# A Sinkhorn-sorted attention followed by a token mixer: Sinkhorn on 128 partitions, another first V, no gates, and a new written-out order

## The chip, the cores and the metric

The kernel runs on one core of a Trainium2 chip. The time is the device time of one execution in microseconds (us); for the kernel before, three runs were taken, and their median is 125.45 us (125.16 to 125.81). The engines are PE (matrix multiply; PEld is its weight load), DVE (vector), ACT (scalar), POOL (GpSimd) and SP (which only issues DMAs here). PE writes to PSUM, eight banks of 128 partitions by 2 KB, and what it has written there is evicted to SBUF by ACT or DVE.

## The reference

There are B=4 batches, H=8 heads, S=768 tokens, D=64 per head, and 8 blocks of 96 tokens.

```python
P = sort_net                                   # (B, H, 8, 8)
for _ in range(5):
    P = exp(P - max(P, axis=-1))
    P = P / (sum(P, axis=-1) + 1e-09)          # rows
    P = P / (sum(P, axis=-2) + 1e-09)          # columns
k_sorted = einsum('bhij,bhjcd->bhicd', P, k_blocks)
v_sorted = einsum('bhij,bhjcd->bhicd', P, v_blocks)
scores = q_block @ k_sorted_block.T / sqrt(D)  # inside each block of 96
attn = exp(scores - max) / (sum + 1e-09)
x = attn @ v_sorted_block                      # -> (B, S, 512), heads side by side
# token mixer
W = (x @ w_q) @ (x @ w_k).T / sqrt(64)
out = relu(W @ x) @ w_out
```

Inputs and output are fp32; the matmuls of the kernel are bf16. The mixer is computed as q (k^T x), so no 768 by 768 matrix is made.

## The kernel before

**Layout.** A token index s is held as s = 6p + r, with p the partition (128 of them) and r from 0 to 5, so a block of 96 tokens covers 16 partitions times 6. The 8x8 matrix P of a head becomes a 128x128 matrix M (tile M, function `u_n`): the block mixing of all 16 partitions of each block at once. One M per head serves all r.

**Units.** The work is cut into some 440 small units. Each is a function `u_X`, and the string ORDER lists every unit in the order in which it is given to its engine; each engine runs its own units strictly in that order. An item such as `K216` is: function K, batch 2, index 1, PSUM bank 6. A small letter is the eviction of the unit of the same name, and its last letter is the engine: `k21A` evicts on ACT, `k21D` on DVE; `P` is POOL, `S` is SP. For a batch:

- `l`: a load. POOL issues a DMA that casts fp32 to bf16 on the way: all of q, k or v of a batch (768 KB written each), into three rotating buffers Qn, Kn, Vn (line 100).
- `Q`/`q`: transposes of q into QT, three units of 16 matmuls, 1024 columns each eviction.
- `K`/`k`: sorted and transposed k into KT, a pair of heads a unit (12 matmuls, 768 columns evicted).
- `V`/`v`: sorted v into Vs, token-major, three units of 8 matmuls and 1024 columns. `R` (line 271): six SP DMAs for each batch that regroup Vs into VT, where the 96 tokens of a block lie on 96 partitions.
- `S`/`e`: scores of five (block, head pair)s, and the exponential on ACT into E (line 301; seven units for a batch, the last with 384 columns, the others with 960).
- `P`, `r`, `x`: E by VT, with a column of ones that gives the sum; reciprocal and product on DVE into X (lines 328 and 333; five units, the last smaller).
- `T`/`t`, `J`/`j`, `W`/`w`, `G`/`g`, `H`/`h`, `O`/`o`, `y`: transposes of X, both projections, the transposed k part, k^T x (tile Ab), the mixed and rectified tile mixT, the output projection (6 units of four 128x512 matmuls; tile ot) and the store by SP (two rows r a store). `d` moves half of qkT to the other partitions (qD), mostly by an SP DMA.

**Sinkhorn** (`u_c`, lines 150 to 163) lies on 32 partitions, one for each (batch, head), with the 8x8 matrix along the free dimension. A round is one exponential on ACT and six DVE instructions: sum, reciprocal and product by rows, then by columns. Behind the fifth round `U`, `b`, `B` and `n` turn P and spread it into M: for batch 0 on DVE, for the others on POOL (`n`), from a copy of the spread P in SBUF (PTR).

**Fillers and gates.** `Z` units multiply zeros (tile fil, 64 matmuls of 128x512 in all) where PE would idle. `N` units are gates: POOL copies one element of a tile, so that it waits there, and the loads behind it in its queue start no earlier.

Of the kernel before, what the change touches and what calls it, by code (L numbers as in the profile page):

```python
# [14 lines left out]

ORDER = """
l00P l01P l02P i00P i03P i02P l11P c00D Z087 c01D i01D c02D Z027 c03D Z127 c04D Q026 Q007 q02D c05D
Q015 Z224 q01A q00D U006 Z423 b00D Z322 B003 n00D u00A Z522 n11P n01D Z622 K010 K032 n10P k01A K024  # L20
k03D Z727 k02A N02k l03P Z1026 V000 V022 v00A K004 v02D V016 k00A N00k l12P l10P Z821 R01S n21P v01D
R00S K112 S000 R04S S044 n20P e00A k11D S066 e06A R02S K100 e04A S012 R05S S036 R03S k10A Z1125 Z924
e03A K120 K134 e01A k12D S026 e02A k13D P002 S050 r00D Z1227 e05A x00D N00x l21P P014 V106 r01D P030
x01D v10A P042 r04D P024 r03D x04D T007 x03D V112 t00A R10S v11A r02D Q106 x02D R11S Q127 T031 q12A
Q110 q10D T015 t03D q11A N11q l20P l31P l04P l32P l30P T024 V122 t01A S100 n31P v12D S156 t02A J005
e10A n30P S122 R12S j00D J014 R15S e15A K200 R14S j01D W005 R13S e12A w00D W014 S116 w01D G005 e11A
K232 G015 k23A K216 g01D k20A k21D S144 P112 e14A P100 r11D K226 x11D P134 k22A r10D Q213 r13D x10D
S166 Q202 q21A x13D T101 q20A Q220 t10D S134 e16A q22D e13A K322 P146 k32D S250 S214 e25A r14D P122
x14D e21A K330 r12D S246 d00S x12D k33A K304 e24A k30D S220 T123 T112 e22A t12D K314 S236 t11D T133
k31A S260 J102 t13D e23A S204 d01S j10D J113 e26A N26e l22P e20A V306 V310 v30D j11A W102 H024 v31A  # L30
W113 w11D V326 w10D h02D G103 v32A H000 d10S R30S Q312 h00D Q325 q31A G113 q32D Q304 g11A H010 O057
q30D h01A S312 o05D S324 e31A S330 O036 R34S e32A R35S V222 o03D R33S O007 e33A v22D R32S d11S V214
R31S V200 o00D v21A R25S S342 O016 R24S v20D e34A R23S H114 R22S O027 o01D R20S R21S H100 P322 o02A
h11D y00S O046 h10A r32D S304 x32D y01S o04A O107 e30A P240 y02S P232 o10A r24D P214 x24D P226 r23D
r21D O131 x23D O120 r22D o13A x21D T233 o12A P201 x22D t23A S364 y11S O110 e36A r20D T223 x20D o11A
T217 P304 t22A y10S T202 r30D t21A H120 x30D J213 t20A P316 j21D h12A S354 J202 r31D d21S x31D e35A
W213 O141 j20D T300 w21D o14A d20S P334 t30D W207 P342 r33D O156 w20D x33D G207 o15A r34D T311 x34D
T320 y12S t31A G217 t32D T336 g21A J301 t33D H222 H214 j30D J310 h22A d30S W301 H206 j31A w30D O243
h20A d31S W312 G301 o24D h21A O250 w31D O227 o25A G311 y22S o22A O230 g31A H302 H324 o23A O211 h32A
y21S H316 O200 o21D O351 h30D h31A O345 o20A o35D O314 y20S o34D O307 o31A y32S O325 o30A O334 y30S  # L40
o32A o33A y31S
# [4 lines left out]
def kernel(  # L46
# [20 lines left out]
    D1 = D + 1  # L67
    DM = moe_w_out.shape[0]
    DH = moe_w_q.shape[1]
    PT = DM // P  # L70
    NU = NB * H
    TH = 5
    NT = -(-NB * NP // TH)
    EW = 2 * TH * BLK + P - BLK
    AG = 14
# [15 lines left out]
    Pm = sb.tile([BH, NB + 1, NB], FP32, name="Pm")  # L91
    nc.sync.dma_start(out=Pm[:, 0:NB, :], in_=sort_net.rearrange("b h i j -> (b h) i j"))
# [6 lines left out]
    def load(t, src, b):  # L99
        nc.gpsimd.dma_start(out=t[b % NIN].rearrange("p h r d -> p h (r d)"),  # L100
                            in_=src[b].rearrange("h (p r) d -> p h (r d)", p=P))

    QT = tiles("QT", 2, [P, NP, R6, P])
    KT = tiles("KT", 2, [P, NP, S + P - BLK])
    Vs = tiles("Vs", 2, [P, R6, H, D1])
    VT = tiles("VT", 2, [BLK, NB, H * D1])
    E = tiles("E", 2, [BLK, NT, EW])
    X = tiles("X", 2, [BLK, NB, DM])
# [6 lines left out]
    NOT = 4  # L115
    ot = tiles("ot", NOT, [P, 2, DM], FP32)
    M = tiles("M", 2, [P, H, SP, NB])
    R = tiles("R", 4, [BLK, 2, 7], FP32)
    PTR = sb.tile([P, NB, BH], BF16, name="PTR")
    Pb = sb.tile([BH, NB, NB], BF16, name="Pb")  # L120
    PbT = sb.tile([NB * NB, BH], BF16, name="PbT")
    Lx = sb.tile([NB * NB, NB, NB, SP], BF16, name="Lx")
    tmp = sb.tile([BH, NB], FP32, name="tmp")
# [4 lines left out]

    Pv = Pm[:, 0:NB, :]

    def rows(t):
        return t.unsqueeze(2).to_broadcast([BH, NB, NB])

    def cols(t):
        return t.unsqueeze(1).to_broadcast([BH, NB, NB])
# [12 lines left out]


    def u_c(b, n, e):  # L150
        if n == 0:
            nc.vector.memset(Pm[:, NB:NB + 1, :], 1e-9)
            nc.vector.memset(fil, 0.0)  # L153
            nc.vector.reduce_max(tmp, Pv, axis=AX.X)
            nc.vector.tensor_sub(Pv, Pv, rows(tmp))
            return
        nc.scalar.activation(Pv, Pv, ACT.Exp)
        nc.vector.reduce_sum(tmp, Pv, axis=AX.X)
        nc.vector.reciprocal(tmp, tmp)
        nc.vector.tensor_mul(Pv, Pv, rows(tmp))  # L160
        nc.vector.reduce_sum(tmp, Pm.rearrange("p i j -> p j i"), axis=AX.X)
        nc.vector.reciprocal(tmp, tmp)
        nc.vector.tensor_mul(Pb if n == 5 else Pv, Pv, cols(tmp))


    def u_i(b, n, e):
        if n == 0:
            nc.gpsimd.memset(idb, 0.0)
            nc.gpsimd.affine_select(out=idb, in_=idb, compare_op=ALU.not_equal, fill=1.0, base=0,
                                    pattern=[[-1, P]], channel_multiplier=1)  # L170
        elif n == 1:
            nc.vector.reduce_max(m_p, idb.rearrange("p (j s) -> p s j", s=SP), axis=AX.X)
        elif n == 3:
            nc.gpsimd.memset(Lx, 0.0)
            nc.gpsimd.affine_select(out=Lx.rearrange("p i j s -> p (i j) s"),
                                    in_=Lx.rearrange("p i j s -> p (i j) s"),
                                    compare_op=ALU.not_equal, fill=1.0, base=0,
                                    pattern=[[-1, NB * NB], [0, SP]], channel_multiplier=1)
        elif n == 2:
            for t in Vs:  # L180
                nc.gpsimd.memset(t[:, :, :, D:D1], 1.0)
            for t in KT:
                nc.gpsimd.memset(t[:, :, S:S + P - BLK], 0.0)
            for t in E:
                nc.gpsimd.memset(t[:, :, 2 * TH * BLK:EW], 0.0)
                nc.gpsimd.memset(t[:, NT - 1, 2 * (NB * NP - TH * (NT - 1)) * BLK:EW], 0.0)


    def u_l(b, n, e):
# [5 lines left out]
        else:  # L195
            load((Qn, Kn, Vn)[n], (q, k, v)[n], b)


    def u_U(b, n, bank):
        mm(bf(bank)[0:NB * NB, 0:BH], Pb.rearrange("p i j -> p (i j)"), idb[0:BH, 0:BH], t=True)  # L200

    def u_b(b, n, e):
        nc.vector.tensor_copy(PbT, bf(U["t"])[0:NB * NB, 0:BH])

    def u_B(b, n, bank):
        for i in range(NB):
            mm(PS[:, bank, i * BH:(i + 1) * BH], Lx[:, i].rearrange("p j s -> p (j s)"), PbT)

    U = {}

    def u_n(b, n, e):
        h0, h1 = n * 4, n * 4 + 4
        if b == 0:
            src = PS[:, U["bank"], 0:NB * BH].rearrange("p (i h) -> p h i", h=BH)
        else:
            src = PTR.rearrange("p i h -> p h i")
        src = src[:, b * H + h0:b * H + h1, :]
        ENG[e].tensor_tensor(  # L218
            out=M[b % 2][:, h0:h1], in0=src.unsqueeze(2).to_broadcast([P, 4, SP, NB]),
            in1=m_p.unsqueeze(1).unsqueeze(3).to_broadcast([P, 4, SP, NB]), op=ALU.mult)  # L220

    def u_u(b, n, e):
        copy(e, PTR.rearrange("p i h -> p (i h)"), PS[:, U["bank"], 0:NB * BH])


    def u_Z(b, n, bank):
        for _ in range(n):
            mm(PS[:, bank, :], fil[:, 0:P], fil)


    def u_Q(b, n, bank):
        ps = bf(bank).rearrange("p (k r s) -> p k r s", k=NP, r=2)
        for r in range(2):
            for kp in range(NP):
                for hh in range(2):
                    mm(ps[hh * D:(hh + 1) * D, kp, r, :], Qn[b % NIN][:, 2 * kp + hh, 2 * n + r, :],
                       idb, t=True)

    def u_q(b, n, e, bank):
        copy(e, QT[b % 2][:, :, 2 * n:2 * n + 2, :].rearrange("p k r s -> p k (r s)"),  # L240
             bf(bank).rearrange("p (k s) -> p k s", k=NP))


    def flat(bank, nb=2):
        return PS[:, bank:bank + nb, :].rearrange("p a n -> p (a n)")

    def u_K(b, n, bank):
        ps = flat(bank)
        for r in range(R6):
            for hh in range(2):  # L250
                h = 2 * n + hh
                mm(ps[hh * D:(hh + 1) * D, r * P:(r + 1) * P], Kn[b % NIN][:, h, r, :],
                   M[b % 2][:, h].rearrange("p s i -> p (s i)"))

    def u_k(b, n, e, bank):
        copy(e, KT[b % 2][:, n, 0:S].rearrange("p (i s r) -> p i s r", i=NB, s=SP),
             flat(bank)[:, 0:S].rearrange("p (r s i) -> p i s r", r=R6, s=SP))


    def u_V(b, n, bank):  # L260
# [209 lines left out]
```

## Time and profile before

| | |
|---|---|
| median of the runs | 125.45 us |
| span of the profiled execution (first to last instruction) | 123.3 us |
| PE busy, its mean granted clock | 101.9 us (83%), 0.934 |
| DVE busy | 69.5 us (56%), 132 instructions |
| ACT busy | 69.2 us (56%), 93 instructions |
| POOL busy | 27.1 us (22%) |
| casting loads (q0) | 10.09 MB written, 56.9% of the DMA engines' time |
| plain DMAs (q1) | 9.89 MB, 24.2% |
| fillers that the profile shows | 60, 17.6 us of PE |

A busy share is a mean over stages with different limits, and PE's busy time counts the depth of the pipeline with each matmul, and fillers too. So the page tells who is busiest and not what sets the time; for that the stretches of the span are read one by one. Granted clock 1.00 is full speed of PE. The page's GB/s count what is written; a casting load reads twice that from memory.

### The profile page before, as it was taken

What the parts mean: (1) busy time and instruction counts of PE and PEld (TensorE: products, weight loads), DVE (VectorE), ACT (ScalarE), POOL (GpSimd) and SP (SyncE); (2) the same over time, 40 slices, a digit from 0 to 9 for tenths busy, and PEclk for the clock granted to TensorE, in tenths of its full rate; (3) what the DMA queues carried; (4) which work ended last, traced back from release to release, by engine and by line L of the source; (5) the groups of instructions that cost most, each with busy time, mean ns of one, the idle gap of its engine ahead of it and who ended that gap; (6) DMA issues with size and microseconds to landing.
All of it is one profiled execution on the core that took longest, in us unless ns stands there. A gap on an engine that the chain in (4) does not pass through costs nothing. (4 is left out here: it accounts for less than half of the span.)

```text
span 123.3 us, 3389 instructions
## 1 busy us (share of the span) xinstructions
PE 101.9 (83%) x1439; PEld 65.7 (53%) x1449; DVE 69.5 (56%) x132; ACT 69.2 (56%) x93; POOL 27.1 (22%) x42
## 2 busy tenths in 40 slices
PE   5818877692799999608998999999999999999940
PEld 2216464541447886508887677554767665443410
DVE  2879547305402976404769669497697885304500
ACT  4113155863301699900579977885669736855550
POOL 6993096910020029900000030000000000000000
PEclk9976999999679999995589999999999999999995
DMA  0999999899949426999999339947947104144493
GB/s 4 141 203 203 205 203 153 142 215 227 147 34 203 106 57 57 196 243 206 206 203 206 54 33 175 260 104 202 396 156 308 53 16 175 32 169 171 167 363 153
DMA packets 19950, 20.19 MB, mean 164 GB/s; under 512 B 2016, under 2 KB 18400, under 8 KB 19936
## 3 DMA queue, kind: packets, MB, share of 16 engines
q0 software_dynamic: 14064, 10.09, 56.9%
q1 hardware_dynamic: 5872, 9.89, 24.2%
q8 instruction: 11, 0.18, 0.6%
q14 instruction: 3, 0.02, 0.1%
HBM read 20.19 MB, written 6.29 MB: 215 GB/s over the span
## 5 line engine op out<-in xcount | busy, mean ns | idle before, releaser
L301 ACT ACTIVATE E<-ps 96x960 bf16<-96x960 f32 (+1 forms) x28 | 24.2, 906 | 7.7 <-PE ps L138 7.6
L138 PE MATMUL ps<-wo,mixT 128*128 128x512 bf16 x90 | 22.6, 380 | 0.6 <-issue 0.2
L333 DVE TENSOR_TENSOR X<-ps,R 96x896 bf16<-96x896 f32 (+1 forms) x20 | 19.7, 998 | 0.5
L138 PE MATMUL ps<-fil 128*128 128x512 bf16 x60 | 17.6, 438 | 2.0 <-DVE fil L153 1.2
L138 PE MATMUL ps<-VT,E 96*128 96x65 bf16 x256 | 11.7, 202 | 7.7 <-DMA VT<-Vs 7.2
L138 PEld LDWEIGHTS <-E 96*128 96x128 bf16 x256 | 10.3, 103 | 9.4 <-issue 8.5
L142 ACT COPY ot<-ps 128x512 f32<-128x512 f32 x16 | 9.4, 585 | 10.1 <-PE ps L138 9.2
L138 PEld LDWEIGHTS <-mixT 128*128 128x128 bf16 x96 | 8.2, 98 | 9.4 <-issue 1.3
L328 DVE RECIPROCAL R<-ps 96x14 f32<-96x14 f32 (+1 forms) x20 | 4.3, 222 | 15.4 <-PE ps L138 15.4
L138 PEld LDWEIGHTS <-fil 128*128 128x128 bf16 x64 | 6.5, 110 | 10.0 <-issue 4.4
L138 PE MATMUL ps<-idb,Qn 128*64 128x128 bf16 x192 | 9.2, 263 | 3.1 <-DMA Qn<-in_q_dram 3.1
L142 ACT CAST KT<-ps 128x768 bf16<-128x768 f32 x9 | 7.1, 800 | 6.8 <-PE ps L138 6.8
L142 ACT CAST Vs<-ps 128x1024 bf16<-128x1024 f32 x6 | 6.2, 1029 | 8.1 <-PE ps L138 7.8
L144 DVE CAST KT<-ps 128x768 bf16<-128x768 f32 x7 | 6.6, 956 | 6.7 <-PE ps L138 6.5
L138 PE MATMUL ps<-M,Kn 128*64 128x128 bf16 x192 | 8.3, 227 | 2.2 <-DMA Kn<-in_k_dram 0.9
L138 PEld LDWEIGHTS <-Qn 128*64 128x64 bf16 x192 | 7.7, 138 | 4.3 <-DMA Qn<-in_q_dram 3.6
L138 PE MATMUL ps<-QT,KT 64*128 64x96 bf16 x256 | 9.8, 207 | 0.2 <-ACT KT L142 0.2
L144 DVE COPY ot<-ps 128x512 f32<-128x512 f32 x8 | 5.5, 689 | 7.6 <-ACT ot L142 4.8
L406 ACT ACTIVATE mixT<-ps 128x1024 bf16<-128x1024 f32 x8 | 8.1, 1029 | 2.7 <-PE ps L138 2.6
L144 DVE CAST Vs<-ps 128x1024 bf16<-128x1024 f32 x6 | 7.2, 1222 | 3.0 <-PE ps L138 3.0
L138 PEld LDWEIGHTS <-Kn 128*64 128x64 bf16 x192 | 6.4, 113 | 4.5 <-issue 2.5
L218 POOL TENSOR_TENSOR M<-PTR,m_p 128x512 bf16<-128x512 bf16 x6 | 7.7, 1321 | 5.0 <-ACT PTR L142 4.9
(67 smaller groups left out, 132.9 us busy)
## 6 DMA issues: line engine op xcount, KB each, us to landing
out_dram<-ot SPq DMA_DIRECT2D x12, 512.0 KB, 2.8
VT<-Vs SPq DMA_DIRECT2D x24, 130.0 KB, 4.6
Qn<-in_q_dram POOLq DMA_DIRECT2D x4, 768.0 KB, 11.0
Kn<-in_k_dram POOLq DMA_DIRECT2D x4, 768.0 KB, 10.9
Vn<-in_v_dram POOLq DMA_DIRECT2D x4, 768.0 KB, 11.5
wo<-in_moe_w_out_dram POOLq DMA_DIRECT2D x1, 512.0 KB, 14.7
qD<-qkT SPq DMA_DIRECT2D x8, 48.0 KB, 2.3
wqk<-in_moe_w_q_dram POOLq DMA_DIRECT2D x1, 64.0 KB, 3.5
```

The costliest lines, as they stand in the source:

```text
L138: nc.tensor.matmul(o, w, x, is_transpose=t, start=start, stop=stop, skip_group_check=True)
L142: nc.scalar.copy(o, i)
L144: nc.vector.tensor_copy(o, i)
L218: ENG[e].tensor_tensor(out=M[b % 2][:, h0:h1], in0=src.unsqueeze(2).to_broadcast([P, 4, SP, NB]), in1=m_p.unsqueeze(1).unsqueeze(3).to_bro ...
L301: nc.scalar.activation(E[b % 2][:, n, 0:2 * w * BLK].rearrange("p (t a c) -> p a t c", a=2, c=BLK), PS[0:BLK, bank:bank + 2, 0:w * BLK].re ...
L328: nc.vector.reciprocal(rr[b, n][:, :, 0:w], avps(bank, w)[:, :, :, D])
L333: nc.vector.tensor_mul(xo.rearrange("p (a t d) -> p a t d", a=2, d=D), avps(bank, w)[:, :, :, 0:D], rr[b, n][:, :, 0:w].unsqueeze(3).to_br ...
L406: nc.scalar.activation(o, i, ACT.Relu)
```

## The change

The diff replaces ORDER whole and changes the units as follows.

- **Sinkhorn** (`c`, `f`, `r`, `C`) lies on 128 partitions, one for each (batch, head, row i) of two batches; two groups (batches 0 and 1; 2 and 3) take turns. Of a round, `f` is the exponential with the row sum as a by-product, `r` reciprocal and product by rows on DVE, `C` two small fp32 matmuls on PE that sum the columns (a block-diagonal matrix of ones, blk, and a rank-one term for the 1e-9), `c` reciprocal from PSUM and product. POOL makes blk with a memset and two selects (`i04P`).
- **M** (`U`, `u`, `m`) comes from one transpose of the spread P for each group; all 16 products for M are on DVE, a pair of heads (256 columns) each.
- **First loads.** The first four heads of q and k of batch 0 are loaded as fp32 by SP into ot, which is free then, and cast head by head (`z`): six on POOL, one on DVE, one on ACT. The other halves, and v in two halves, are casting loads.
- **First V.** For batch 0 (TURNED) v is sorted and transposed like k, into VS (in the same memory as Vs), then turned back by eight PE transposes for a pair of heads (`A`) and evicted into VT (`a`, 1024 columns). Batch 0 has no `R` any more.
- **Pairs.** Q, S, P, X, T and J go by head pairs: Q and T are four units of 768 columns, J gathers as T units come, W turns all 128 columns where it turned 64.
- **Output.** ot is one tile with eight slots; the last batch's last two rows are stored singly.
- **Gates and fillers.** No gate is left in ORDER, and of the fillers 17 (13 of 128x512, 4 of 128x128), all ahead of `U001`.

```diff
-l00P l01P l02P i00P i03P i02P l11P c00D Z087 c01D i01D c02D Z027 c03D Z127 c04D Q026 Q007 q02D c05D
...
+i03D c00D l06S l05S i15P f01A r01D l08P i00P i01D i04P l07P f11A Z050 C010 c01D r11D f02A r02D
+Z031 Z111 C020 c02D f03A C111 c11D r03D z05P f12A r12D Z032 C031 l010P c03D f04A r04D C120 c12D
+f13A Z022 Z132 C041 c04D f05A r05D Q020 C051 q02A z00D Q032 l09P c05D z04P U001 r13D C130 z03A
+m01D V013 z01P c13D z02P m00D u00D q03A m03D v01A Q012 z06P z07P V005 q01D K010 V033 f14A r14D
+C142 v00D k01A m02D S020 v03A c14D A017 e02A A003 a00D f15A V024 a01D K000 K022 m10D r15D v02A
+Q006 q00D K034 A037 l10P i02P m12D k00A S010 k02A A022 k03A a03D S064 e01A a02D S046 Q113 q11D
...
+x00D v10A R11S V112 v11A P010 x01D P034 V126 v12A R14S R12S R15S x03D S032 e03A T000 U101 l11P
+K126 u10A K104 k12A K112 R13S k11A R10S t00D l03P k10D P040 x04D K136 k13A P024 S122 e12A S156
+T030 e15A m20D i25P S142 x02D T024 t03D t02D T015 t01D S136 e14A S110 e13A e11A m22D J002 J012
...
+J106 J116 J126 J136 R22S S204 j11D j10A H012 m33D h01A e20A l32P R20S R25S P240 x24D m31D W106
...
-    Pm = sb.tile([BH, NB + 1, NB], FP32, name="Pm")
+    Pm = sb.tile([P, 2, NB], FP32, name="Pm")
+    nc.sync.dma_start(out=Pm, in_=sort_net.rearrange("(g b) h i j -> (b h i) g j", g=2))
...
+    def u_c(g, n, e, bank=None):
...
+        c, p1, o = cs[:, g, :], Pm[:, g, :], Ue[:, g, 0:NB]
+        nc.vector.reciprocal(c, PS[:, bank, 0:NB])
+        if n == 5:
+            c, p1 = (t.unsqueeze(2).to_broadcast([P, NB, SP]) for t in (c, p1))
+            o = Pf[g]
+        nc.vector.tensor_mul(o, p1, c)
+
+    def u_f(g, n, e):
+        nc.scalar.activation(Uf[:, g, :], Ue[:, g, :], ACT.Exp, accum_out=rs[:, g:g + 1])
+
+    def u_r(g, n, e):
+        nc.vector.reciprocal(rs[:, g:g + 1], rs[:, g:g + 1])
+        nc.vector.tensor_scalar_mul(Pm[:, g, :], Uf[:, g, 0:NB], rs[:, g:g + 1])
+
+    def u_C(g, n, bank):
+        mm(PS[:, bank, 0:NB], eps[:, 0:P], eps[:, P:P + NB], stop=False)
+        mm(PS[:, bank, 0:NB], blk, Pm[:, g, :], start=False)
...
+    def u_m(b, n, e, bank):
...
+        ENG[e].tensor_tensor(
+            out=M[b % 2][:, 2 * n:2 * n + 2],
...
+    def u_z(b, n, e):
+        t = (Qn, Kn)[n // 4][0][:, n % 4].rearrange("p r d -> p (r d)")
+        src = ot.rearrange("p a n -> p (a n)")[:, n * R6 * D:(n + 1) * R6 * D]
...
     def u_V(b, n, bank):
+        if b in TURNED:
+            sort_turn(b, n, bank, Vn)
+            return
...
+    def u_A(b, n, bank):
+        ps = bf(bank).rearrange("p (i d) -> p i d", d=P)
+        for i in range(NB):
+            mm(ps[0:BLK, i, :], VS[b % 2][:, n, i * BLK:(i + 1) * BLK], idb, t=True)
+
+    def u_a(b, n, e, bank):
+        copy(e, VT[b % 2][:, :, 2 * n:2 * n + 2, 0:D],
+             bf(bank)[0:BLK].rearrange("p (i h d) -> p i h d", i=NB, h=2))
```

## The prediction

> **What bounds the kernel now.** I read the stretches of the span first (time, busy time per engine with the number of instructions in brackets, granted clock, DMA share, rate), cut where the behaviour changes.
>
> ```profile
> 24.00:31.20 7.20, 4.27 (x49) 2.26 (x49) 1.82 (x2) 3.55 (x5) 1.01 (x1) 1.00 1.25 221
> 31.20:38.50 7.30, 7.06 (x46) 3.39 (x48) 1.33 (x2) 0.97 (x1) 1.11 (x2) 0.77 0.79 108
> 51.30:55.80 4.50, 0.02 (x1) 0.00 (x0) 0.54 (x1) 1.10 (x2) 1.22 (x1) 1.00 1.24 238
> 55.80:62.20 6.40, 6.35 (x100) 5.40 (x102) 3.66 (x6) 2.49 (x3) 0.00 (x0) 0.50 1.28 205
> 62.20:72.30 10.10, 9.73 (x209) 7.67 (x208) 7.54 (x13) 9.28 (x13) 1.08 (x2) 0.98 0.84 132
> 72.30:118.60 46.30, 45.41 (x549) 26.42 (x552) 30.44 (x49) 31.18 (x43) 0.04 (x1) 1.00 0.58 173
> ```
>
> The columns are PE, weight loads, DVE, ACT, POOL. From 72.3 on PE is dense and sets the pace. Before that there are holes, and DVE and ACT starve with PE. The waits and PE in order of time say what the holes are:
>
> ```profile
> PE ps L138 <- DMA VT<-Vs: 7.2, 2, 4.5
> ...
> 24.21 3.18 PE L138 MATMUL ps<-fil 128*128 128x512 bf16 x13 [0.18 <-ACT E L301]
> ...
> 31.23 0.61 PE L138 MATMUL ps<-VT,E 96*128 96x65 bf16 x14 [2.72 <-DMA VT<-Vs]
> ...
> 33.04 5.60 PE L138 MATMUL ps<-fil 128*128 128x512 bf16 x20 [0.22 <-issue]
> ...
> 55.85 1.70 PE L138 MATMUL ps<-VT,E 96*128 96x65 bf16 x28 [4.53 <-DMA VT<-Vs]
> ...
> 112.38 6.22 PE L138 MATMUL ps<-wo,mixT 128*128 128x512 bf16 x27
> ```
>
> Both holes are the sorted V of a batch, regrouped by six DMAs from Vs to VT. For batch 0 PE idles or runs fillers from 24.2 to 38.5; for batch 1 it idles 4.5 us and then runs at half clock until 62.2. So the span is four pieces: 15.0 to the first sorted matmul (Sinkhorn and M), 57.3 with holes, 46.3 dense, 4.7 from the last matmul to the end (last eviction and stores): 123.3. The median of the runs is 125.45, so 2.15 lie outside the span; I add them to every sum.
>
> **The dense piece, priced.** In it, start-to-start times give PE prices per unit: O (4 matmuls) 0.94, P of 14 about 0.48, G 0.56, T 0.37, J 0.71 per four, V 0.52, S of 10 0.32, Q 0.41 and K 0.46 per 12, H 0.28, W 0.20. Summed over the units that stand behind W of batch 1 in the old order they make 46.4 us, against 46.3 measured. So PE prices carry over.
>
> In the new order I cut at the first P of batch 2. Behind it stand 23 O (21.6), 10 P (4.4), 3 V, 4 K, 6 G (3.4), 8 T, 7 S, 9 H, the J and 6 W: **44.6 us** of PE work, with 30 us each for ACT and DVE. That is the old dense piece again: 44.5. The last stores are split finer (two of 256 KB); I leave 4.7 for the tail.
>
> **Between the new M and that cut: the evictions bind.** All fillers behind U, both VT waits of batch 0 and the gates go. PE has 38.9 us here, among it the new 32 transposes that turn batch 0's V: 32 by 0.062 (the 128-wide V matmul with its weight load) is 2.0. ACT has 21 exponentials (18 by 0.975, 3 by 0.489: 19.0), 9 KT by 0.80 (7.2), 3 turned V by 0.80 (2.4), 6 Vs by 1.03 (6.2), 4 QT by 0.81 (3.2, the 768-wide XT row), 2 mixT (2.1) and 3.2 of small ones: **43.3**. DVE has 10 X with reciprocals (12.2), 11 QT and 8 XT by 0.555 (10.5), 15 M, 4 KT or V by 0.956 (3.8), 4 VT by 0.68 (2.7, the 1024-wide bf16 row), qkT, mixT and half a Sinkhorn (6): about **41**. The M products were POOL's; no row has one of 256 columns on DVE, but 512 columns took 0.692 there, so at most that and at least 0.21 (the small product): I take 0.35. Relevant rows:
>
> ```profile
> L301 ACT ACTIVATE E<-ps 96x960 bf16<-96x960 f32 x24 | 22.6, 975 | 7.7 <-PE ps L138 7.6
> L333 DVE TENSOR_TENSOR X<-ps,R 96x896 bf16<-96x896 f32 x16 | 17.0, 1076 | 0.4
> L142 ACT COPY XT<-ps 128x768 bf16<-128x768 bf16 x8 | 6.1, 810 | 1.3 <-PE ps L138 1.3
> L144 DVE COPY XT<-ps 128x768 bf16<-128x768 bf16 x8 | 4.4, 555 | 2.9 <-PE ps L138 2.9
> ```
>
> So the late one here is ACT, with DVE close behind. The best stretch above ran ACT at 9.28 of 10.1 and both together at 16.8 of 10.1. From below: ACT at 97%, 44.7 us. From above: both at the pair's rate 1.665, 84.3/1.665 = 50.6. I take 90%: **48.2**, against 57.3 today.
>
> **Up to M.** One round was exp, three DVE steps by rows, three by columns; it came every 1.77 us. Now it is exp 0.26 (which also gives the row sum), reciprocal 0.19, product 0.21, two matmuls on PE, reciprocal 0.19, product 0.21: 1.06 and the matmuls, with four handoffs instead of two (two took about 0.2: 0.4). Small fp32 matmuls have no row. From below the 32x32 transpose, 0.20 for both; from above each four filler weight loads at half clock (0.15), 1.2 for both; nearest is the small transpose with a second matmul and its load behind it, 0.5. Round: 1.96. Five from 3.0 (the first exp began at 2.93, and the loads ahead of it differ only in shape) end at 12.8; transpose, first M and handoffs 0.8: 13.6 (today Pb is ready at 12.6, K starts at 15.04). Behind the DVE reciprocal that waits for PE stand the other group's steps, which ACT's next exp waits for; the other group has until batch 2.
>
> One thing is added in this time: POOL casts six heads of q and k (128x384, between 0.6, its memset of 608 columns, and 1.0, three quarters of its 512-wide product) while DVE iterates. The trace has the clash:
>
> ```profile
> 5.56 1.50 POOL L175 TENSOR_SCALAR_AFFINE_SELECT Lx<-Lx 64x1024 bf16<-64x1024 bf16 x1
> ...
> 6.23 0.86 DVE L163 TENSOR_TENSOR Pm<-Pm,tmp 32x64 f32<-32x64 f32 x1
> ```
>
> The product took 0.86 instead of 0.21 and ended with POOL's instruction; reductions and reciprocals beside it kept their time. POOL reads for six casts and two selects (0.29 each), 4 to 5 of the 11 us, so about 40%; ten products on the path, each held for half a cast (0.33) in those: at most 1.3, at least 0; I take 0.5. M's first use: **14.1**, between 12.6 and 18.
>
> The Trainium skill, SBUF — State Buffer, section "SBUF: two separate sides", speaks against this part: it calls the port pair of DVE and GpSimd an exclusive lock, held for a whole instruction, also by a DVE operation with two SBUF inputs when GpSimd reads SBUF. By that rule only the column products (SBUF twice) would be held for certain, some 0.7 us in all, and the sum would be 0.2 longer.
>
> **Loads.** Casting loads wrote 10.09 MB (20.2 read) in 56.9% of the engines' time, 2.8% per MB read; plain ones 9.89 MB in 24.2%, 2.4%. So fp32 halves cost the DMA engines the same and only start earlier, on SP, whose next issue is far off. 4.7 MB at twice 205 GB/s are 11.5 us: the last half lands near 15, V's first half near 11; both are hidden under Sinkhorn, and uncovered cost 1.9 per half. POOL issues batch 1 after the casts and memsets; its memset into Vb waits for batch 0's turned V, and behind it stand only the loads of batches 2 and 3. VT of batch 1: issued by about 33 (ACT's work up to the third Vs), due at 42.7 (up to its first P); landing took
>
> ```profile
> DMA to landing us min/median/max: 2.3/4.6/8.3
> ```
>
> under today's loads. That is priced at nothing, with 1.4 us of cover over the worst.
>
> **Sum:** 14.1 + 48.2 + 44.5 + 4.7 = 111.5; with 2.15, **113.6**.
>
> **The rivals.**
> 1. *The evictions pack tightly and the loop is short:* 12.6 + 44.7 + 43.5 + 4.7 + 2.15 = 107.7. For it: ACT reached 92% while PE was the bound. Against: DVE is as full, and each bank passes PE, ACT or DVE and PE again in a fixed order.
> 2. *The Sinkhorn loop over PE is long and PE starts cold:* M at 18, and the first matmuls at half clock, as after the holes: +3.9, and +1.6 as half of what the 6.4 us at clock 0.50 lost; 119.1. For it: only 17 fillers instead of 64, and a gap on PE in each round. Against: the old start, with 3 us of idle PE, was at full rate by 12.8 (four fillers in 1.04). The Trainium skill, TensorE: Matmul & The Clock Gate, section "What's actually happening", asks for one busy window of about 3.4 us; the estimate from it is 1.7 us lost, 119.2.
> 3. *Slower: without gates VT of batch 1 starves.* From about 24 all remaining loads stand in POOL's queue. If the six transfers got through only when it runs dry (9.3 MB at 0.205 plus 3.8 for the fp32 halves, from 3: 52.2), P waits 9.5 us from 42.7, then runs half speed for 6.4 (3.2 lost): 126.3. It decides once landing takes over 19 us. For it: the 4.5 us hole fell into 238 GB/s of loads. Against: VT landed in 8.3 at most, while that queue stayed full to 66.
>
> **How the numbers follow.** Forecast (110.5 to 117) 0.54, rival 1 0.17, rival 2 0.19 (117 to 123), rival 3 0.10. Range 107 to 121: it leaves out rival 3, the slow end of 2 and the fast end of 1, some 0.18. A difference under 0.5% can't be told from none. Faster 0.87, same 0.03, slower 0.10, the last two from rival 3 and a little of rival 2.
>
> **What would show it.** Right: no filler behind the first sorted matmul, that one near 14, ACT about 90% busy to the first P of batch 2 near 62, then PE dense for 44 to 45. Wrong: PE waiting for VT; DVE products of 0.8 us on the Sinkhorn path; granted clock 0.5 behind M; ACT and DVE both idle between 20 and 60; a dense piece over 47.

## The result, and the profile after

The changed kernel takes 112.25 us (median of four, 111.19 to 113.88) against 125.48 (125.16 to 125.81) in the same comparison: a ratio of 0.890, between 0.884 and 0.896. The profiled execution took 112.5, its span is 110.8. Some kernels below have single executions that lie 2 to 5% above their fastest; of those the range is given, and readings are taken from the profiled execution.

The span cut where the prediction cut it, and at the edges of one hole (columns as before: time, then PE, weight loads, DVE, ACT, POOL busy with their counts, granted clock, DMA share, rate):

```profile
0.00:17.92 17.92, 16.35 (x75) 10.92 (x75) 8.27 (x39) 5.58 (x20) 12.29 (x31) 1.00 1.01 196
17.92:42.65 24.73, 23.48 (x514) 20.20 (x513) 21.24 (x49) 21.65 (x32) 8.40 (x11) 1.00 1.30 199
42.65:45.47 2.82, 0.07 (x4) 0.00 (x1) 0.79 (x2) 1.24 (x2) 0.00 (x0) 0.90 1.28 222
45.47:52.00 6.53, 6.53 (x90) 6.43 (x92) 3.99 (x7) 2.56 (x4) 0.00 (x0) 0.52 1.28 207
52.00:64.83 12.83, 12.11 (x285) 9.36 (x285) 11.21 (x20) 10.46 (x14) 0.00 (x0) 1.00 0.98 181
64.83:106.24 41.41, 40.98 (x526) 25.89 (x532) 29.41 (x48) 29.41 (x44) 0.00 (x0) 1.00 0.44 157
106.24:110.80 4.56, 0.00 (x1) 0.00 (x0) 0.00 (x0) 0.58 (x1) 0.00 (x0) 0.89 0.55 213
```

| piece, us | before | predicted | after |
|---|---|---|---|
| to the first sorted matmul | 15.0 | 14.1 | 17.9 |
| to the first P of batch 2 (before: to the first W of batch 1) | 57.3 | 48.2 | 46.9 |
| dense piece | 46.3 | 44.5 | 41.4 |
| tail | 4.7 | 4.7 | 4.6 |
| outside the span | 2.15 | 2.15 | 1.7 |
| sum | 125.45 | 113.6 | 112.5 |

The total came within 1.4 us, by pieces that miss in both directions: the start is 3.8 longer than forecast, and the next two are 1.3 and 3.1 shorter. The start is now slower than the old one, too. The waits of PE and three rows of its order of time show the one hole that is left:

```profile
PE ps L133 <- DMA VT<-Vb: 2.8, 1, 2.8
...
32.66 5.42 SPq L307 DMA_DIRECT2D VT<-Vb  x6
...
45.47 0.95 PE L133 MATMUL ps<-VT,E 96*128 96x65 bf16 x14 [2.76 <-DMA VT<-Vb]
...
DMA to landing us min/median/max: 2.3/5.9/8.0
```

The hole of batch 0 and its fillers are gone, 7.2 us of waiting in both batches became 2.8, and batch 1 still waits: its six regrouping DMAs are issued one after the other over 5.4 us, the last near 37.5, and that lands about 8 later. The window behind it has 0.52 of the clock for 6.5 us, as the old hole had.

The start is told by one Sinkhorn round, the fourth of the first group, from its row product (11.53) to the next exponential (14.27), and by the head of the round behind it:

```profile
11.36 1.33 PE L133 MATMUL ps<-fil 128*128 128x512 bf16 x5
...
11.53 0.42 DVE L171 TENSOR_SCALAR Pm<-Uf,rs 128x8 f32<-128x8 f32 x1
...
12.62 0.59 PE L133 MATMUL ps<-eps 1*128 1x8 f32 x2
13.14 0.60 PE L133 MATMUL ps<-Pm,blk 128*128 128x8 f32 x2
...
13.77 0.21 DVE L160 RECIPROCAL cs<-ps 128x8 f32<-128x8 f32 x1 [1.38 <-PE ps L133]
14.01 0.17 DVE L164 TENSOR_TENSOR Ue<-Pm,cs 128x8 f32<-128x8 f32 x1
...
14.27 0.21 ACT L167 ACTIVATE Uf<-Ue 128x9 f32<-128x9 f32 x1 [1.49 <-DVE Ue L164]
...
14.39 0.19 ACT L167 ACTIVATION_READ_ACCUMULATOR Uf<-Ue 128x1 f32 x1
...
14.61 0.17 DVE L170 RECIPROCAL rs<-rs 128x1 f32<-128x1 f32 x1 [0.43 <-ACT Uf L167]
14.81 0.48 DVE L171 TENSOR_SCALAR Pm<-Uf,rs 128x8 f32<-128x8 f32 x1
```

Each of the two matmuls of a column sum is two instructions ("x2") and occupies PE for 0.52, start to start: the pair takes 1.05, where 0.5 was predicted. The product is ready at 11.95, but five fillers hold PE until 12.62. The row sum is a second instruction of ACT, 0.19. The exponentials of the first group start at 2.95, 5.17, 7.81, 10.99 and 14.27: rounds of 2.2, 2.6, 3.2 and 3.3, where 1.96 was predicted. Each pair of one group also stands in PE's queue ahead of work of the other.

### The profile page after: what moved, and what is told of

Same layout as the page of the kernel before. It is cut to its first block, busy times and chain, and to the rows that moved or that the text cites. A ratio compares the mean times of both kernels' runs of the same rounds, so it can differ in the third digit from the quotient of the medians.

```text
span 110.8 us, 3517 instructions
## 1 busy us (share of the span) xinstructions
PE 99.5 (90%) x1482; PEld 72.8 (66%) x1491; DVE 74.9 (68%) x162; ACT 71.5 (65%) x115; POOL 20.7 (19%) x41
## 4 chain that ended last, share of the span: by engine, by line
PE 75%; DMA 7%; ACT 5%; DVE 3%; SPq 3%; issue 2%; DVEq 0%; ACTq 0%
PE ps L133 75%; DMA VT<-Vb 7%; SPq L307 3%; ACT Vb L137 3%; ACT E L337 1%; DVE VT L139 1%; ACT QT L137 1%; DVE Pm L171 1%; ACT ot L137 1%; DVE QT L139 0%; DVE M L189 0%; ACT Uf L167 0%; DVE fil L210 0%; DVE rs L170 0%; DVE cs L160 0%
## 5 line engine op out<-in xcount | busy, mean ns | idle before, releaser
L137 ACT CAST Vb<-ps 128x1024 bf16<-128x1024 f32 (+1 forms) x12 | 11.2, 964 | 8.0 <-PE ps L133 8.0
L137 ACT CAST KT<-ps 128x768 bf16<-128x768 f32 x12 | 9.2, 813 | 1.2 <-PE ps L133 1.2
L133 PE MATMUL ps<-QT,KT 64*128 64x96 bf16 x256 | 8.8, 204 | 0.8 <-ACT E L337 0.4
L133 PEld LDWEIGHTS <-KT 64*128 64x128 bf16 x256 | 6.3, 94 | 3.7 <-issue 2.4
L167 ACT ACTIVATE Uf<-Ue 128x9 f32<-128x9 f32 x10 | 2.1, 208 | 10.2 <-DVE Ue L164 7.6
L438 DVE TENSOR_SCALAR mixT<-ps 128x1024 bf16<-128x1024 f32 x6 | 7.3, 1221 | 1.4 <-PE ps L133 1.4
L133 PE MATMUL ps<-fil 128*128 128x512 bf16 (+1 forms) x17 | 6.6, 549 | 1.3 <-DVE fil L210 1.3
L139 DVE COPY XT<-ps 128x768 bf16<-128x768 bf16 x13 | 6.9, 550 | 1.0 <-PE ps L133 0.7
L133 PE MATMUL ps<-idb,X 96*128 96x96 bf16 x128 | 7.0, 206 | 0.0
L133 PEld LDWEIGHTS <-X 96*128 96x128 bf16 x128 | 5.9, 98 | 1.3 <-issue 0.6
## 6 DMA issues: line engine op xcount, KB each, us to landing
Qn<-in_q_dram POOLq DMA_DIRECT2D x3, 768.0 KB, 12.4
```

What stands on the lines that cost most here:

```text
L133: nc.tensor.matmul(o, w, x, is_transpose=t, start=start, stop=stop, skip_group_check=True)
L137: nc.scalar.copy(o, i)
L139: nc.vector.tensor_copy(o, i)
L167: nc.scalar.activation(Uf[:, g, :], Ue[:, g, :], ACT.Exp, accum_out=rs[:, g:g + 1])
L438: nc.vector.tensor_relu(o, i)
```

## The experiments

Each kernel is the changed kernel with one edit. They ran on three chips, each beside its own runs of the kernel before: medians 125.8, 124.4 and 124.0, single runs from 122.4 to 127.4. Times from two chips differ by that too, so the verdicts rest on places in the traces.

### What makes the start long

**One sum** (the pair replaced by one matmul; the 1e-9 in the column sums is left out):

```diff
-        mm(PS[:, bank, 0:NB], eps[:, 0:P], eps[:, P:P + NB], stop=False)
-        mm(PS[:, bank, 0:NB], blk, Pm[:, g, :], start=False)
+        mm(PS[:, bank, 0:NB], blk, Pm[:, g, :])
```

> Leaves out the 1e-9 in the column sums: one fp32 matmul a round and group instead of two. Theory (PE's column sums make the start long: in the changed kernel each of the two matmuls held PE 0.52 us, and the first sorted matmul came at 17.9): 0.5 us less in each of five rounds and 0.5 less just ahead of the first V, so first sorted matmul at 14.8 to 15.5, and 1.5 to 3 us off the whole, some of it eaten by the wait for VT of batch 1 if that is set by the loads. Rival (products on DVE held by POOL's casts are what is long): the start falls by under 1 us, the whole by under 1.

109.39 us (108.46 to 110.08), ratio to before 0.874 (0.863 to 0.885). The last transpose of the start, U, comes at 13.51 instead of 16.66: 3.15 us for five pairs that lost about half a microsecond each (2.6), and for the other group's pairs ahead of them in PE's queue, which lost as much. The first sorted matmul gained only 1.95 (15.97), for a reason that the fold below shows as well.

**One group** (the second group's rounds moved behind the first sorted matmul; an extract):

```diff
-i03D c00D l06S l05S i15P f01A r01D l08P i00P i01D i04P l07P f11A Z050 C010 c01D r11D f02A r02D
+i03D c00D l06S l05S i15P f01A r01D l08P i00P i01D i04P l07P Z050 C010 c01D f02A r02D
```

> The second Sinkhorn group (batches 2 and 3) starts only when the first is through. Theory (group 0 also waits in the in-order queues behind group 1: its column sums on PE, its c on DVE ahead of group 0's r): first sorted matmul 1 to 2 us earlier than 17.9, since three pairs of column sums of 1.05 us leave PE's queue ahead of it and one DVE wait of 0.7; the whole 0.5 to 2 us faster. Rival (a round is long by itself, 2.2 us as its first one was): first sorted matmul by 0.5 us or less earlier, the whole unchanged.

The first sorted matmul came at 15.14, 2.8 earlier, so the other group in the queues is a cost of that size. But the first P came at 30.98, 0.8 later than in the changed kernel: the work of its five rounds reappeared among the evictions. The profiled execution took 111.61, the other three 115.2 to 115.6. Moving the rounds brings nothing.

**Five fillers** (12 of the 17 removed, items Z):

> Twelve of the 17 fillers, all those behind the first column sum, are left out. Theory (at half clock they hold PE's queue when group 0's third and fourth column sums are ready, 0.3 and 0.7 us): first sorted matmul near 17.0 instead of 17.9, the whole 0.5 to 1 us faster; the clock, half until about 20.5 in the changed kernel, rises no later than 21.5. Rival (the fillers are what brings the clock up): full clock only at 23 or later, the whole 0.5 to 2 us slower.

112.07 (111.42 to 112.78), as the changed kernel. The trace shows two effects that cancel: the first sorted matmul came at 16.11, 1.8 earlier, yet the first P at 30.80, 0.6 later. The second part is the clock; it is read below.

**The fold** (one matmul, and the 1e-9 kept: an eighth of it added to each of the eight terms of a column):

```diff
-        nc.vector.tensor_scalar_mul(Pm[:, g, :], Uf[:, g, 0:NB], rs[:, g:g + 1])
+        nc.vector.tensor_scalar(out=Pm[:, g, :], in0=Uf[:, g, 0:NB], scalar1=rs[:, g:g + 1],
+                                scalar2=EPS / NB, op0=ALU.mult, op1=ALU.add)
...
-        mm(PS[:, bank, 0:NB], eps[:, 0:P], eps[:, P:P + NB], stop=False)
-        mm(PS[:, bank, 0:NB], blk, Pm[:, g, :], start=False)
+        mm(PS[:, bank, 0:NB], blk, Pm[:, g, :])
```

> The column sum is one matmul, as in the run with one sum, but the 1e-9 is kept: an eighth of it is added to each of the eight terms in the DVE product before (a second scalar operation of the same instruction). Theory (the two-matmul column sum is the largest part of the long start, and a second scalar operation costs the instruction nothing): the first sorted matmul near 16, the time 109.4 (108.5 to 110.5), as with one sum. Rival (the instruction with two scalars is longer, 0.1 to 0.2 in each of ten rounds): near 110.5 to 111.

109.76 (109.0 to 110.15), ratio 0.891 (0.882 to 0.900). The first sorted matmul came at 16.04 and the first P at 27.97 (30.16 in the changed kernel), and the product with two scalars still takes 0.23 where nothing holds it. This computes everything and is the shortest complete version of this study. All its four times lie below all four of the changed kernel, 2.5 us in the medians, but the two were not run beside each other, and their ratios to before are the same (0.891 and 0.890); so the times do not settle it, and what the traces show is a first P 2.2 us earlier. What keeps it from 14 is this, in its order of time:

```profile
13.33 0.89 POOL L240 DMA_DIRECT2D Qn<-in_q_dram  x1
...
13.58 0.29 PE L133 MATMUL ps<-idb,Pf 128*128 128x128 bf16 x1 [0.18 <-DVE Pf L164]
13.63 1.76 DVE L171 TENSOR_SCALAR Pm<-Uf,rs 128x8 f32<-128x8 f32 x1
13.91 1.49 DVE L189 TENSOR_TENSOR M<-ps,m_p 128x256 bf16<-128x256 bf16 x1
14.21 0.68 POOL L203 MEMSET VT<- 96x64 bf16 x2
14.46 0.68 POOL L205 MEMSET KT<- 128x128 bf16 x2
15.06 0.30 POOL L207 MEMSET E<- 96x224 bf16 x1
...
15.54 0.57 PE L133 MATMUL ps<-Pm,blk 128*128 128x8 f32 x2 [1.67 <-DVE M L189]
16.04 0.85 PE L133 MATMUL ps<-M,Vn 128*64 128x128 bf16 x12
```

A product of the other group, 0.23 elsewhere, lasts 1.76 and ends at 15.39, among POOL's memsets; it began 0.6 before the first of their rows, while POOL issued a load. M stands behind it in DVE's queue and ends with it at 15.4, and PE waits 1.67. That the memsets are what holds it is inferred, from such rows and from where the holds went when the memsets moved.

**The memsets moved.** To take that hold off M, they were put behind the second K cast, where POOL idled from 9.0 to 11.4, and the other group's sum behind the first sorted matmul, with the fold:

```diff
-f13A Z022 Z132 C041 c04D f05A r05D Q020 C051 q02A z00D Q032 l09P c05D z04P U001 r13D C130 z03A
-m01D V013 z01P c13D z02P m00D u00D q03A m03D v01A Q012 z06P z07P V005 q01D K010 V033 f14A r14D
+f13A Z022 Z132 C041 c04D f05A r05D Q020 C051 q02A z00D Q032 l09P c05D z04P i02P U001 r13D z03A
+m01D V013 C130 z01P c13D z02P m00D u00D q03A m03D v01A Q012 z06P z07P V005 q01D K010 V033 f14A r14D
...
-Q006 q00D K034 A037 l10P i02P m12D k00A S010 k02A A022 k03A a03D S064 e01A a02D S046 Q113 q11D
+Q006 q00D K034 A037 l10P m12D k00A S010 k02A A022 k03A a03D S064 e01A a02D S046 Q113 q11D
```

> One column-sum matmul with the 1e-9 kept in the product, the memsets behind the second K cast, and the other group's column sum behind the first sorted matmul. Theory (with one sum, the first M was held 1.1 us beside POOL's memsets and PE waited 1.7 for it): first sorted matmul near 14.2, the time 107.5 to 108.5. Rival (the memsets hold the products of the late rounds for as long as they held M): 109 to 110, no better than the one fold alone.

The rival held, and more: 110.02 to 112.83, first sorted matmul at 17.68, 1.6 later than with the fold alone. The hold went where the memsets went, into the rounds:

```profile
8.64 1.56 DVE L171 TENSOR_SCALAR Pm<-Uf,rs 128x8 f32<-128x8 f32 x1
9.02 0.68 POOL L203 MEMSET VT<- 96x64 bf16 x2
...
10.78 0.28 POOL L207 MEMSET E<- 96x224 bf16 x1
...
11.06 2.49 DVE L171 TENSOR_SCALAR Pm<-Uf,rs 128x8 f32<-128x8 f32 x1
...
12.57 0.96 POOL L225 CAST Kn<-ot 128x384 bf16<-128x384 f32 x2
13.47 0.89 POOL L240 DMA_DIRECT2D Qn<-in_q_dram  x1
```

The second product began as the last memset did (11.06 and 11.12) and was freed at 13.55, when POOL had also done the four casts that followed without a gap (13.53). A cast alone need not do this: with the fold, a product that began inside a cast (11.73) took 0.23. Why one is caught and another not was not settled.

### The loads

**Casting loads** (q and k of batch 0 by casting DMAs again, no casts on the engines):

> The fp32 loads of the first q and k and the eight casts are undone: all six halves are casting loads from POOL's queue. Theory of the held products: DVE products on the Sinkhorn path return from 0.3 to 0.48 us to about 0.2, the start is 0.9 us shorter, first sorted matmul near 17.0, and the whole about 1 us faster. Rival (the fp32 loads pay, because they start earlier and the queue of POOL is slow): products change little on the path, some load of batch 0 is late, PE waits for Qn or Kn, and the whole is 0.5 to 2 us slower.

112.86 (111.86 to 113.41), ratio 0.901 (0.890 to 0.912). The first sorted matmul came at 17.66, 0.26 earlier, and PE waited for no load of batch 0. So the fp32 loads and their casts cost the start next to nothing, and bring it nothing. The memsets, which follow POOL's loads directly there, held a product for 0.98 at 8.66.

**The memsets early** (the same move as above, without the fold):

> Only POOL's memsets of the padding move: from behind the Q load of batch 1 to behind the second K cast, where POOL was idle from 9.0 to 11.4. The loads of V and K of batch 1 are then issued near 14 and 15 instead of 16.9 and 17.7. Theory (no load binds before VT of batch 1, and that VT is late because all loads slow it): 112.3 (111.5 to 113), the memsets hold DVE by up to 1 us in the fourth or fifth round instead. Rival (earlier loads leave the DMA engines free sooner, so VT lands sooner): 110 to 111.

111.26 to 114.35; first sorted matmul 18.02, and PE waits 2.9 for VT of batch 1, as in the changed kernel. V and K of batch 1 were issued near 14 and 15, 3 us earlier, and nothing came of it: no load binds there.

### The first V

**Six DMAs again** (batch 0 no longer in TURNED; its A and a units replaced by R; an extract):

```diff
-TURNED = (0,)
+TURNED = ()
```

> V of batch 0 goes by Vs and six transfers into VT, as in the kernel before; all else is as changed. Theory of the prediction (the holes of batch 0 were that detour): V is evicted at about 20 to 24, the transfers land about 8 us later, at 30 to 33, the first P, at 30.2 in the changed kernel, waits 1 to 4 us, and half clock follows if it is over 3; the whole 2 to 6 us slower. Rival (the new order gives PE enough other work until then, and the detour saves 2.0 us of PE and 2.7 of DVE): wait under 1 us, the whole within 1 us, and the old holes came from the old order and its gates.

121.09 (120.47 to 121.65), ratio 0.974 (0.967 to 0.981): 8.8 above the changed kernel, with the first P at 35.49 instead of 30.16. But PE did not wait for VT of batch 0 there (0.2 at most). POOL's memset of VT had to wait for the regrouped first V, and the loads of batch 1 behind it came 14.5 us late; PE waited 1.9 for KT, whose memset stood behind that of VT, and later 2.2 for Vn, and it ran at the low rate of the start until about 35.5 (24 transposes at 33.58 took 1.49, 0.86 in the changed kernel). So it was repeated with the memsets early, to be held against the kernel just before:

> Batch 0's V is regrouped by six DMAs again, and the memsets stand where the last kernel has them, so that nothing in POOL's queue waits for VT of batch 0 (in the earlier run with these DMAs POOL waited 14.7 us for it and the loads of batch 1 were 14 us late). To be held against the last kernel. Theory (the detour of the first V itself is what the old kernel paid): first P near 35, the time 5 to 9 above the last kernel's, 117 to 121. Rival (most of the 9 us of the earlier run were the late loads of batch 1): 2 to 4 above it, 114 to 116.5.

116.04 (115.45 to 117.23), 2.4 above the median of that kernel (113.6), which is the rival's band. But that kernel's four times lie between 111.26 and 114.35; by the shortest of each (115.45 and 111.26) it is 4.2, between the bands of rival and theory, so the run does not decide between them. Here are POOL's memset and the next load in the first of the two, and the first P in the second:

```profile
28.73 0.66 POOL L203 MEMSET VT<- 96x64 bf16 x2 [14.65 <-DMA VT<-Vb]
...
31.36 0.87 POOL L240 DMA_DIRECT2D Vn<-in_v_dram  x1
```

```profile
32.94 0.59 PE L133 MATMUL ps<-VT,E 96*128 96x65 bf16 x14 [0.84 <-DMA VT<-Vb]
```

The first P comes at 32.94 against 32.60, and waits 0.84, where the kernel before waited or ran fillers from 24.2 to 38.5. Both executions are of those in which PE reaches its full rate late (at 29.1 and 27.2; see the clock of PE below). In the changed kernel, where it came at 21.2, the first P began at 30.16, and transfers that land at 32.9 would have cost it up to 2.8. So turning V on PE is worth between 1.3 us (the spans, 113.4 and 112.1, both with the late rate) and 4.2, and 5.0 of the 8.8 went when the memsets moved. The new order gives PE and ACT other work until VT is there, and that removes a good part of the old hole; how much of it is the order and how much the turned V, these runs do not settle.

### VT of batch 1

**A gate** (POOL waits for VT of batch 1 before it issues the loads behind V of batch 2):

```diff
-l20P Q216 q21A Q224 q22D l21P Q205 q20A Q237 q23D K212 k21A K230 k23D K204 k20A K226 k22D S222
+N10t l20P Q216 q21A Q224 q22D l21P Q205 q20A Q237 q23D K212 k21A K230 k23D K204 k20A K226 k22D S222
```

> One gate put back: POOL issues the loads behind V of batch 2 only when the last transfer into VT of batch 1 has landed. Theory (the 2.8 us that PE waited for VT and the 6.5 us at clock 0.52 behind it come from loads that share the DMA engines with VT's six transfers): VT lands by 42.7, the wait is under 0.5 us, no half-clock stretch at 45 to 52, 3 to 6 us off the whole unless Q or K of batch 2 is now late. Rival (six transfers take 8 us whatever is beside them): the wait stays 2 us or more, and the whole is unchanged or slower.

114.71 to 116.93. The wait for VT is gone, and the price is these waits, below a stretch in which the DMA engines did nothing:

```profile
PE ps L133 <- DMA Kn<-in_k_dram: 4.3, 1, 4.3
PE ps L133 <- DMA Qn<-in_q_dram: 1.6, 1, 1.6
...
40.00:42.00 2.00, 2.00 (x37) 1.42 (x35) 1.89 (x5) 2.00 (x3) 1.08 (x3) 1.00 0.01 4
```

So the loads do slow the regrouping (median landing 3.2 with the gate, 5.9 without, over all eighteen DMAs), and the loads have no slack to give: 2.8 us of waiting became 5.9.

**V of batch 1 on PE as well** (TURNED = (0, 1), its six R replaced by four A and their evictions):

> V of batch 1 too is sorted and turned on PE, as that of batch 0: its six transfers into VT are gone, PE gets 32 transposes (2.0 us) and DVE four evictions (2.7 us) more. Theory (the 2.8 us that PE waited for VT of batch 1 and the 6.5 us at clock 0.52 behind cost 6 us, and nothing else stands there): no wait for VT of batch 1, clock 1.00 from 45 to 52, the added work of 2 to 3 us given back, 2 to 4 us off the whole. Rival (the loads fill the DMA engines until 57, so the wait only moves on to Q or K of batch 2, as it did with the gate, where PE waited 1.6 and 4.3 us for them): a wait for Qn or Kn of 2 us or more, and the whole within 1 us of the changed kernel.

117.15 (115.84 to 118.37), ratio 0.937 (0.926 to 0.948), so worse by some 5, and neither theory was right. No load was late; the turned pieces went through one bank, each transpose behind the eviction of the last, and PE's queue stood behind them:

```profile
PE ps L133 <- DVE VT L139: 1.4, 3, 0.7
PE ps L133 <- ACT Vb L137: 1.3, 1, 1.3
...
ACT E L337 <- PE ps L133: 10.6, 10, 3.4
```

Batch 1's first P came at 52.3, after 45.5 with the DMAs and their wait. About 2 of these 6.8 us are the late clock told of next. Another 2.7 are a second stretch of half clock, which the theory did not have: from 46.7 to 52.3 the granted clock was 0.51, though no VT was waited for. In it, the four J units of batch 0 took 2.74, and 1.46 in the changed kernel:

```profile
48.94 2.74 PE L133 MATMUL ps<-XT,wqk 128*128 128x384 bf16 x8
```

What is left for the transposes and their one bank is about 2 us more than the DMAs' wait of 2.8. With one sum as well, that stretch came again (from 43.2 on), and the result was the same:

> Both: one column-sum matmul a round (leaves out the 1e-9 in the column sums) and V of batch 1 turned on PE. If the two gains are of different stretches they add: about 3 us from the first (measured alone: 109.4 against 112.25), 2 to 4 from the second, 105 to 107. If the loads bind up to 57 us, the second adds nothing here: 109 to 110, with PE waiting for Qn or Kn of batch 2.

111.84 to 117.22, above one sum alone.

### The clock of PE at the start

In every trace the matmuls run at a low rate at first. Where the full rate begins was read off PE's order of time, here first in the changed kernel and then in the one with casting loads, whose start was 0.26 earlier:

```profile
20.48 0.77 PE L133 MATMUL ps<-M,Vn 128*64 128x128 bf16 x12
21.18 0.38 PE L133 MATMUL ps<-eps 1*128 1x8 f32 x2
...
22.13 1.09 PE L133 MATMUL ps<-idb,Vb 128*96 128x128 bf16 x16
23.16 0.53 PE L133 MATMUL ps<-M,Vn 128*64 128x128 bf16 x12
```

```profile
20.22 0.85 PE L133 MATMUL ps<-M,Vn 128*64 128x128 bf16 x12
21.00 0.59 PE L133 MATMUL ps<-eps 1*128 1x8 f32 x2
...
22.56 1.94 PE L133 MATMUL ps<-idb,Vb 128*96 128x128 bf16 x16
24.43 0.85 PE L133 MATMUL ps<-M,Vn 128*64 128x128 bf16 x12
```

The sixteen transposes of the turned V take 1.09 in the one and 1.94 in the other, twelve matmuls behind them 0.53 and 0.85. Nine kernels read so:

| profiled execution | first sorted matmul | full rate from | first P | first sorted to first P |
|---|---|---|---|---|
| changed kernel | 17.9 | 21.2 | 30.2 | 12.2 |
| one sum | 16.0 | 20.4 | 28.1 | 12.1 |
| fold | 16.0 | 20.3 | 28.0 | 11.9 |
| gate | 18.1 | 21.9 | 30.6 | 12.4 |
| fold, memsets early | 17.7 | 22.3 | 30.4 | 12.7 |
| five fillers | 16.1 | 25.4 | 30.8 | 14.7 |
| casting loads | 17.7 | 26.9 | 32.2 | 14.6 |
| memsets early | 18.0 | 27.2 | 32.6 | 14.6 |
| V of batch 1 on PE | 18.1 | 26.6 | 32.3 | 14.2 |

In these nine the full rate begins 3 to 5 us after the first sorted matmul, or 8 to 10, and the late ones reach the first P 2.3 us later (the mean of the last four, 14.5, less that of the first five, 12.3). Of the other four, whose order differs more, one group has it 3 us after the first sorted matmul, one sum with V of batch 1 on PE some 5 to 6, the six DMAs with the memsets early 10, and the six DMAs 17. This is how five fillers won 1.8 at the start and lost it again by the first P, and why casting loads can't be told from the fp32 loads by the total. The column of the granted clock shows 1.00 in these stretches, so it doesn't tell.

What decides between early and late was not tried by itself. In the late ones a column-sum pair came at the low rate some 3.3 us after the first sorted matmul; in the changed kernel that pair was already at the full rate, and the fold's single matmul at 19.4, still at the low one, did no harm. But the work of PE alone does not decide: the gate and V of batch 1 on PE have the same groups of matmuls at the same times, to 0.01 us, from 13.14 up to that pair (21.47 and 21.46), and from there on one is early and the other late.

The half clock behind the wait for VT of batch 1 varies as well. Read in steps of 0.5 us, the granted clock is about 0.5 for 6.8 us in the changed kernel (wait 2.8), for 3.4 in seven others (waits 2.0 to 3.2), and not at all in one group (2.4) and with the six DMAs (3.0). At half clock 6.8 us lose 3.4, so a difference of that size between two profiled executions need not come from the edit: of the 3.3 by which the span of one sum is shorter, 2.1 stands at the first P, and 1.7 can be this. It also goes with a part of the scatter: the profiled execution of one group had a mean granted clock of 1.00 and took 111.61, the other three, at 0.94 to 0.96, took 115.2 to 115.6. What decides here isn't shown either.

## Why the prediction was right

**Right in the total and in the sign, by sums that cancel.** The forecast of 113.6 was 1.35 above the median. The change does what it says: no filler behind the first sorted matmul, no wait for VT of batch 0, PE dense from the first P of batch 2. That one came at 64.8, near the 62 forecast. But one of its own signs of being wrong came too, PE waiting for VT, and ACT was busy for 77% (35.9 of 46.9) and not for 90% up to there.

**The start: the column sum was mis-sized.** "The small transpose with a second matmul and its load behind it, 0.5" was the nearest row, and the upper bound, 1.2 from the weight loads at half clock, was nearly the truth: 1.05. That is 0.55 in each of five rounds, 2.75 in all; taking one matmul away moved U by 3.15. The rest is the other group's pairs in PE's queue (2.8 when that group is gone, though in part the same microseconds) and the fillers (1.8). "Four handoffs" priced neither. Held products cost little in the changed kernel (0.37 to 0.48 in place of 0.2 in five rounds, near 1) and up to 2.5 where memsets met them.

**The evictions: they did not bind, and a wait was priced at nothing.** ACT's 43.3 of work behind the first sorted matmul was 35.9 (21.65 + 1.24 + 2.56 + 10.46 in the windows). One exponential, one QT and one mixT lay in other pieces (2.8 by their rows). The rows that are left add up to 40.3, count by mean, and where they stand back to back they overlap, by 4.4 in all:

```profile
31.55 2.85 ACT L137 CAST Vb<-ps 128x1024 bf16<-128x1024 f32 x3
...
38.12 5.77 ACT L337 ACTIVATE E<-ps 96x960 bf16<-96x960 f32 x7 [0.47 <-PE ps L133]
```

Seven exponentials in 5.77 are 0.82 each, not 0.975; three evictions of V 0.95, not 1.03. ACT was busy for 88% of the stretch ahead of the hole (21.65 of 24.73) and 82% of the one behind it (10.46 of 12.83), but PE for 95% and 94% (23.48 and 12.11), and of the chain that ended last PE holds 75% of the span and ACT 5%. So "the late one here is ACT" failed as the step that sets this piece. PE's own terms come closer: its 38.9 of the forecast, 1.4 for the low rate until 21.2 (twelve matmuls every 0.64, 0.36 to 0.39 later), 2.8 of waiting and 3.3 for half clock are 46.4, an estimate, against 46.9. That ACT's share gave 48.2 is luck: without the hole and its half clock the piece would be 40.8, below the lower bound of 44.7.

ACT does stand on the path at one place: from 29.1 to 34.4 the chain runs over its exponentials and the three evictions of V, and then over the six transfers. There "VT of batch 1: issued by about 33" failed. That is where the first of six was issued; each holds SP for 0.55 to 1.1, the last left near 37.5, and landed when due plus 2.8. The hole and the half clock behind it (6.53, half of it lost, 3.3) cost 6.1. The due time itself, 42.7, was met to 0.1.

**The dense piece: prices fitted too high.** They were taken from start to start in the old dense piece, 0.9 of which PE was not busy, and were mis-sized: the piece has the units of the forecast, and PE is busy for 40.98 of 41.41, where 44.6 was summed. The largest part is O:

```profile
99.15 7.09 PE L133 MATMUL ps<-wo,mixT 128*128 128x512 bf16 x31
```

These last eight O take 7.09, 0.89 each, and all 23 from start to start 20.2 where 21.6 was priced. The scores, G and K are each 0.3 to 0.7 below their price by the same reading; H of a batch is 0.76 where three by 0.28 were priced, and P of 14 about 0.45 instead of 0.48.

**The rivals.** The second had the mechanism of the start and nearly its size: 17.9 where it said 18, and the low rate behind M, until 21. It was offset elsewhere, so its time, 119.1, did not come. The third's mechanism came true in the small, 2.8 of wait instead of 9.5, because VT landed in 8 and not in 19. The first had its dense piece and fast evictions, not its short loop.

## What to carry to other kernels

Price a small fp32 matmul by rows of its own, at the rate PE runs at then (two instructions and 0.52 here), not by the nearest small bf16 row, and see whether a constant term can go into an instruction that is there anyway. When several small DMAs must all land, count from the issue of the last, not the first. A piece of a kernel is worth what its replacement loses in the same order: the first V's detour seemed worth 9 us until the loads behind it were freed, and then 1.3 to 4.2. Before a difference of 2 or 3 us between two profiled executions is put down to an edit, see where each has PE's low rate and half clock.

## What was not expected of the hardware

- An fp32 matmul of 8 columns appears as two instructions and takes 0.52 at the low rate of the start and 0.32 later, start to start. The Trainium skill, FP8 and Floating Point Precision, section "TensorE Precision Notes", speaks of four passes for true fp32; the rows here show two instructions, and no run tells how many passes lie in one.
- DVE's fp32 product of 128x8 with one tensor input, 0.2 alone, took 0.98 to 2.49 beside POOL's memsets, whose rows are 0.28 to 0.73. The Trainium skill, SBUF — State Buffer, section "SBUF: two separate sides", has a lock held for one instruction at a time, which concerns DVE operations in a two-port mode, and those with two SBUF inputs where POOL reads. The rows do not say in which mode the product runs; but the hold of 2.49 began with the last memset (11.12 to 11.72) and outlasted it by four casts.
- PE reached its full rate 3 to 5 or 8 to 10 us after the first sorted matmul in the nine kernels of the table, with PE nearly always busy. The Trainium skill, TensorE: Matmul & The Clock Gate, section "What's actually happening", has one busy window of about 3.4 us; the early ones (3.3 to 4.6) are near it, the late ones (8.5 to 9.3) are not.
- Behind a wait for VT of 2.0 to 3.2 us PE had half clock for 6.8 us, for 3.4 or not at all, and the length of the wait does not tell which: none came behind 3.0, and 3.4 behind 2.0.
